# The start of a fused convolution and MLP kernel: absolute values, softmax steps and weight loads issued in another order

## The chip, the cores and the metric

One core of one Trainium2 chip runs the whole kernel. The metric is the device time of one execution in microseconds (us), the median of several runs; lower is better.

The engines that matter: TensorE (PE, its weight loads are PEld) multiplies matrices into PSUM; VectorE (DVE) and ScalarE (ACT) do elementwise work; SyncE (SP) issues most DMAs and GpSimd (POOL) a few. Each engine works through its own instructions strictly in the order in which they were issued, and waits where one of them needs a result of another engine.

## The reference

```python
w = softmax(weight_gen, axis=-1)                 # (4, 4096, 8, 7)
x_unf = causal windows of 7 rows of x            # x: (4, 4096, 192)
out = einsum('bshk,bskhg->bshg', w, x_unf)       # a convolution with weights per position and head
h = out.reshape(16384, 192) @ w_in               # (192, 2048)
g = s * relu(h)**2 + b
result = g @ w_out                               # (2048, 192)
```

Weights arrive as doubles (pairs of 32-bit words); the rest is float32.

## The kernel before

The 16384 tokens are cut into 32 groups of 512. For each group the convolution is worked out in "pieces" (softmax, products with the seven taps, sums, a transposition, a split of the result in a high and a low part), and then the MLP runs over the 2048 hidden columns. Precision comes from splitting: weights and activations are held as a high and a low part in the fp32r format, and the products high x high, low x high and high x low are added up in PSUM.

The hidden columns are cut into eight chunks of 256 (`wc[0]` to `wc[7]`). In the first group each chunk's weights have to be converted from doubles before they can be used. `convert(i)` is a generator of four steps, and `ahead(i, n)` runs the next n steps of chunk i:

1. ScalarE takes the absolute value (L228) into the tile `t`, once all of the chunk's weights have landed.
2. VectorE clamps and shifts it (L231, L235) and puts the float together in `r` (L239); ScalarE casts the high part (L243).
3. VectorE takes the exponent (L246) and scales the low word into `v` (L250). `t` is free after that.
4. TensorE forms the low part in PSUM (L260 to L262), ScalarE casts it (L263).

The first group runs as eight turns of a loop, i = 0 to 7 (L681 on). Turn i is: first product of chunk i on TensorE (`mm1_pair`, L527); ScalarE takes relu (L556), square (L558) and, after the low part of chunk i+1 (L263), the cast `gh` (L562); step 2 and 3 of chunk i+2 and step 1 of chunk i+3; second product of chunk i-1 (`mm2_pair`, L596), which alternates `gh` and `gl` as operands; pieces of the second group's convolution as the table `beside` says; then VectorE's `gl` (L568) for chunk i. So on TensorE the order is: first product of i, conversion of i+1 (L260), second product of i-1.

The order in the program is the order on each engine (`manual_schedule`). The pieces of a group are numbered 0 softmax_a (L382, L384), 1 exp (ACT, L390), 2 softmax_b (L395 to L399), 3 to 6 products (L413), 7 to 10 sums (L424), 11 last sum (L432), 12 transposes (L443, L448), 13 split_hi (two ACT casts, L455), 14 split_lo (two DVE subtractions, L461, and DMAs). After turn 7 the column sums of the second weights go to PSUM (L296, in the tile tagged h1), VectorE makes `bias` from them (L304, L305), and the steady loop starts with `mm1_quad` (L545), whose second output again needs the buffer h1.

In the steady loop each step n does the first product of a pair of chunks (`mm1_quad`, L545), relu and square, the second product of the pair before (`mm2_quad`, L614, which works on output tiles 0 and 2 first and then on 1 and 3), and pieces of the next group. At the start of a group, `scale` (L626, L632) brings the outputs of the group before from PSUM to SBUF, which also frees the four PSUM banks for the new group.

Weights come in pairs of chunks, `load_weights(k)`, into two buffers `r`: four transfers of first weights (L189), eight small ones (L198, on the queue named `side`), and one or two of second weights (L206).

Pair 1 is loaded right after pair 0 and the second group's `weight_gen`; pair 2 overwrites the buffer of pair 0 and so is issued when chunk 1 has been read.

Of the kernel before, what the change touches and what calls it, by code (L numbers as in the profile page):

```python
# [20 lines left out]
def dynamic_conv_then_relu2_mlp(  # L21
# [28 lines left out]
    P = 128  # L50
# [24 lines left out]
    rows = ctx.enter_context(tc.tile_pool(name="rows", bufs=1))  # L75
# [5 lines left out]
    yp = ctx.enter_context(tc.tile_pool(name="yp", bufs=2))  # L81
    ps_h = ctx.enter_context(tc.tile_pool(name="ps_h", bufs=1, space=bass.MemoryType.PSUM))
# [136 lines left out]
    def convert(i):  # L219
# [6 lines left out]
        t = raw.tile([P, CW], U32, tag="t", name="t", bufs=1)  # L226
# [38 lines left out]

    spare = const.tile([P, 16], F32, name="spare")
# [220 lines left out]
    def run_pieces(g, a, b):  # L487

        if g < NG:
            if g not in pieces_t:  # L490
                pieces_t[g] = conv_pieces(g)
            for f in pieces_t[g][a:b]:
                f()
# [159 lines left out]
    with tc.manual_schedule():  # L653
        constants()
        nc.scalar.activation(out=spare[:, 0:1], in_=ones_f[:, 0:1], func=AF.Exp)
        load_rows(0)
        load_weights(0, (0,), nc.gpsimd)
        load_weights(0, (1,), nc.gpsimd)
        load_gen(1)
        load_weights(1)  # L660
# [6 lines left out]
        def ahead(i, n):  # L667
            for _ in range(n if i < NC else 0):
                next(parts[i])
# [10 lines left out]
        beside = ((2, 4), (4, 5), (5, 7), (7, 8), (8, 10), (10, 12), (12, 14), (14, 15))  # L680
        for i in range(NC):  # L681
            n, p = divmod(i, 2)
            mm1_pair(n, p, (0, 2, 1) if i == 0 else (0, 1, 2))
            if i == 0:
                ahead(1, 2)
            relu2(n, [p], lambda: ahead(i + 1, 1))
            if i == 0:
                ahead(2, 1)
                run_pieces(1, 0, 2)
            ahead(i + 2, 2)  # L690
            ahead(i + 3, 1)
            if i == NC - 1:
                sums = column_sums()
            if i > 0:
                mm2_pair((i - 1) // 2, (i - 1) % 2)
            run_pieces(1, *beside[i])
            low_g(n, p)
            if i == 0:
                load_weights(2)
            if i == NC - 1:  # L700
                set_bias(sums)
            if i == 1:
                load_weights(3)
            if i == 4:
                load(2)
        run_pieces(2, 0, 3)
        last = NG * NQ - 1
        for n in range(NQ, last + 1):
# [14 lines left out]
            if k == 0:  # L723
                scale(g - 1, (0, 2, 1, 3))
                store(g - 1, 0, NT)
            low_g(n, 1)
# [38 lines left out]
```

## Time and profile before

| | |
|---|---|
| median of 3 runs | 1182.03 us (1180.51 to 1182.61) |
| the profiled execution's own time | 1182.32 us |
| its span in the trace | 1180.6 us |
| TensorE matmul busy | 99% of the span |
| VectorE, ScalarE busy | 79%, 70% |
| DMA, mean over the span | 43 GB/s |

The span is the time from the first instruction to the last; the execution's own time lies 1.7 us above it. TensorE is busy nearly all the time, so what it still waits for is looked up in the view of waits, and where that happens in the timeline.

### The profile page before, as it was taken

To read this page: it belongs to the slowest core of one execution; us is meant where nothing else is said; L and a number is where in the kernel's file an instruction comes from. 1 tells how busy PE (TensorE), PEld (TensorE's weight loads), DVE (VectorE), ACT (ScalarE), POOL (GpSimd) and SP (SyncE) were. 2 spreads that over 40 slices of the span, in tenths; PEclk is the share of its full clock that TensorE was granted. 3 is DMA by queue.
4 is the path that set the end of the run, shared out by engine and by line. 5 is a ranking of instruction groups with operands and counts; after the bars stand their busy time and mean duration, and the time that the engine had idled before them with its cause. 6 is when DMAs were issued, how large, how long until landed. Compare 5 with 4: busy or idle time off the path is not lost.

```text
span 1180.6 us, 30020 instructions
## 1 busy us (share of the span) xinstructions
PE 1163.3 (99%) x12736; PEld 1047.2 (89%) x12736; DVE 931.9 (79%) x1356; ACT 828.1 (70%) x894; POOL 13.9 (1%) x38
## 2 busy tenths in 40 slices
PE   7999999999999999999999999999999999999997
PEld 5688998998999999989989999999899899999996
DVE  7978887777888777798777788777788877788843
ACT  5767776776776767767767767677677677677674
POOL 2000000000000000000000000000000000000000
PEclk9999999999999999999999999999999999999999
DMA  7411122222112222112222112222212222211110
GB/s 191 106 32 37 32 38 47 46 33 46 25 36 46 46 33 46 27 34 46 46 36 42 31 34 42 46 46 33 41 28 38 46 46 33 46 25 36 24 24 15
DMA packets 171290, 50.36 MB, mean 43 GB/s; under 512 B 160212, under 2 KB 163924, under 8 KB 171156
## 3 DMA queue, kind: packets, MB, share of 16 engines
q1 hardware_dynamic: 170644, 48.18, 21.9%
q8 instruction: 100, 1.64, 0.6%
q0 software_dynamic: 512, 0.26, 0.1%
q14 instruction: 34, 0.28, 0.1%
HBM read 27.70 MB, written 12.58 MB: 34 GB/s over the span
## 4 chain that ended last, share of the span: by engine, by line
PE 95%; DVE 1%; ACT 1%; DMA 1%; SPq 1%; issue 0%; DVEq 0%
PE po L614 47%; PE ph L545 44%; PE po L596 2%; PE ph L527 1%; DMA r<-in_moe_w_in_dram 1%; PE ph L260 1%; DVE gl L568 0%; ACT r L558 0%; SPq L198 0%; SPq L189 0%; ACT gh L562 0%; ACT r L556 0%; PE ph L296 0%; DMA r<-in_moe_w_out_dram 0%; SPq L122 0%
## 5 line engine op out<-in xcount | busy, mean ns | idle before, releaser
L614 PE MATMUL po<-wc,gh 64*128 64x384 f32 x3936 | 571.7, 356 | 0.0
L614 PE MATMUL po<-wc,gl 64*128 64x192 f32 x3936 | 495.2, 248 | 0.8 <-DVE gl L568 0.8
L568 DVE TENSOR_TENSOR gl<-r,gh 128x1024 fp32r<-128x1024 f32 x256 | 313.0, 1223 | 222.4 <-ACT gh L562 214.3
L556 ACT ACTIVATE r<-ph 128x1024 f32<-128x1024 f32 x256 | 249.1, 1024 | 311.9 <-PE ph L545 302.7
L614 PEld LDWEIGHTS po<-wc,gl 64*128 64x128 f32 x3936 | 375.5, 187 | 6.4 <-DVE gl L568 1.0
L614 PEld LDWEIGHTS po<-wc,gh 64*128 64x128 f32 x3936 | 369.7, 184 | 5.4
L545 PE MATMUL ph<-xa,wc 64*128 64x512 f32 x2976 | 369.8, 394 | 0.0
L545 PEld LDWEIGHTS ph<-xa,wc 64*128 64x128 f32 x2976 | 270.6, 185 | 55.0 <-issue 0.2
L562 ACT CAST gh<-r 128x1024 fp32r<-128x1024 f32 x256 | 268.8, 1050 | 7.9
L558 ACT ACTIVATE r<-r 128x1024 f32<-128x1024 f32 x256 | 270.8, 1058 | 0.3
L545 PE MATMUL ph<-xb,wc 64*128 64x512 f32 x1488 | 192.2, 390 | 0.0
L413 DVE TENSOR_TENSOR pr<-xt,w 128x1536 f32<-128x1536 f32 (+1 forms) x124 | 187.6, 1553 | 1.3
L545 PEld LDWEIGHTS ph<-xb,wc 64*128 64x128 f32 x1488 | 139.7, 184 | 32.8
L424 DVE TENSOR_TENSOR pr<-pr 128x1536 f32<-128x1536 f32 (+1 forms) x124 | 140.7, 1155 | 2.1
L626 DVE SCALAR_TENSOR_TENSOR u<-po,s_sb,bias 128x192 f32<-128x192 f32 x128 | 49.8, 409 | 1.6 <-PE po L596 1.6
L632 DVE SCALAR_TENSOR_TENSOR y<-po,s_sb,u 128x192 f32<-128x192 f32 x128 | 49.7, 408 | 0.1
L432 DVE TENSOR_TENSOR acc<-pr 128x768 f32<-128x768 f32 x31 | 29.7, 958 | 1.1
L443 DVE STREAM_TRANSPOSE xT<-acc 128x128 f32<-128x128 f32 x124 | 27.6, 280 | 1.0
L448 DVE STREAM_TRANSPOSE xT<-acc 128x128 f32<-128x128 f32 x124 | 26.3, 269 | 0.0
L596 PE MATMUL po<-wc,gh 128*128 128x384 f32 x80 | 25.5, 379 | 0.1
L596 PE MATMUL po<-wc,gl 128*128 128x192 f32 x80 | 21.1, 264 | 3.4 <-DVE gl L568 3.4
L461 DVE TENSOR_TENSOR xa<-xT,xa 128x512 fp32r<-128x512 f32 x31 | 21.2, 685 | 0.0
(60 smaller groups left out, 351.7 us busy)
## 6 DMA issues: line engine op xcount, KB each, us to landing
xt<-in_x_dram SPq DMA_DIRECT2D x120, 132.0 KB, 3.3
out_dram<-y SPq DMA_DIRECT2D x124, 96.0 KB, 1.9
xb<-xb SPq DMA_DIRECT2D x124, 64.0 KB, 2.3
wg<-in_weight_gen_dram SPq DMA_DIRECT2D x124, 28.0 KB, 2.6
r<-in_moe_w_out_dram SPq DMA_DIRECT2D x8, 384.0 KB, 3.6
r<-in_moe_w_in_dram SPq DMA_DIRECT2D x12, 128.0 KB, 3.1
r<-in_moe_w_in_dram SPq DMA_DIRECT2D x24, 32.0 KB, 1.9
xr<-in_x_dram SPq DMA_DIRECT2D x1, 672.0 KB
```

The source lines that it names most:

```text
L413: nc.vector.tensor_tensor(out=pr[:, k0:k1, :, h * G:(h + 1) * G], in0=bass.AP(xs.tensor, xs.offset, [xs.ap[0], [FQ, n], [FQ, J], [1, G]]), ...
L424: nc.vector.tensor_tensor(out=pr[:, o:o + n], in0=pr[:, o:o + n], in1=pr[:, a:a + n], op=ALU.add)
L432: nc.vector.tensor_tensor(out=acc, in0=pr[:, 0], in1=pr[:, 2], op=ALU.add)
L545: nc.tensor.matmul(out=h_t[n, p][:, j], lhsT=w1(2 * k + p, part, block, j, rows), rhs=v[rows], start=(at < 2 and c == 0), stop=(at >= 4 an ...
L556: nc.scalar.activation(out=r[p], in_=h_t.pop((n, p)), func=AF.Relu)
L558: nc.scalar.activation(out=r[p], in_=r[p], func=AF.Square)
L562: nc.scalar.copy(out=gh, in_=r[p])
L568: nc.vector.tensor_tensor(out=gl, in0=sq, in1=gh.bitcast(F32), op=ALU.subtract)
L596: nc.tensor.matmul(**m)
L614: nc.tensor.matmul(**m)
L626: nc.vector.scalar_tensor_tensor(out=u[i], in0=o_t[g][tiles[i]][:, 1, :], scalar=s_sb, in1=bias, op0=ALU.mult, op1=ALU.add,)
L632: nc.vector.scalar_tensor_tensor(out=y[:, t], in0=o_t[g][t][:, 0, :], scalar=s_sb, in1=u[i - 1], op0=ALU.mult, op1=ALU.add,)
```

## The change

- Odd chunks take their tile `t` (step 1 of a conversion) from the pool `rows`; so even and odd chunks have a buffer each, where there was one. The pool `rows` is made after the others.
- Step 1 of chunk 2 is issued ahead of relu of turn 0, and ahead of the cast of chunk 1's high part.
- In turn 1 the first product takes its operands in the order high x high, high x low, low x high, as turn 0 already did; the low part of the weights is needed last.
- The second group's pieces are spread anew over the eight turns: turn 0 does only softmax_a; exp and softmax_b are in turn 1, and turn 6 does the last three sums, the transposes and split_hi.
- The weights of pair 1 are issued on SP ahead of the second group's `weight_gen`; the eight small transfers of pair 2 are issued by POOL.
- The scaling of the first group's output is split in two halves, tiles 0 and 2, then 1 and 3; the second `gl` stands between them.
- The dummy exp that loads ScalarE's table writes to `bias` in place of a tile of its own.

```diff
-    rows = ctx.enter_context(tc.tile_pool(name="rows", bufs=1))
...
     yp = ctx.enter_context(tc.tile_pool(name="yp", bufs=2))
+    rows = ctx.enter_context(tc.tile_pool(name="rows", bufs=1))
...
-        t = raw.tile([P, CW], U32, tag="t", name="t", bufs=1)
+        t = (rows if i % 2 else raw).tile([P, CW], U32, tag="t", name="t", bufs=1)
...
+        load_weights(1)
         load_gen(1)
-        load_weights(1)
...
-        beside = ((2, 4), (4, 5), (5, 7), (7, 8), (8, 10), (10, 12), (12, 14), (14, 15))
+        beside = ((0, 1), (1, 3), (3, 4), (4, 5), (5, 7), (7, 8), (8, 14), (14, 15))
         for i in range(NC):
             n, p = divmod(i, 2)
-            mm1_pair(n, p, (0, 2, 1) if i == 0 else (0, 1, 2))
+            mm1_pair(n, p, (0, 2, 1) if i < 2 else (0, 1, 2))
             if i == 0:
+                ahead(2, 1)
                 ahead(1, 2)
             relu2(n, [p], lambda: ahead(i + 1, 1))
-            if i == 0:
-                ahead(2, 1)
-                run_pieces(1, 0, 2)
...
-                load_weights(2)
+                load_weights(2, side=nc.gpsimd)
...
-            if k == 0:
+            if n == NQ:
+                scale(0, (0, 2))
+                low_g(n, 1)
+                scale(0, (1, 3))
+                store(0, 0, NT)
+            elif k == 0:
                 scale(g - 1, (0, 2, 1, 3))
                 store(g - 1, 0, NT)
-            low_g(n, 1)
+            if n > NQ:
+                low_g(n, 1)
```

ScalarE at the start of the loop, before. `wc_0` to `wc_3` are the chunks' converted weights, `r_121` holds chunks 0 and 1, `r_153` chunks 2 and 3; L228 is step 1, L243 the high part, L263 the low part, L556 to L562 are relu, square and `gh`, L390 is exp.

```order
L243 CAST wc_0_91<-r_121 128x768
L228 ACTIVATE t_289<-r_121 128x768
L263 CAST wc_0_91<-ph_291 128x768
L243 CAST wc_1_92<-r_121 128x768
L556 ACTIVATE r_319<-ph_299 128x1024
L558 ACTIVATE r_319<-r_319 128x1024
L263 CAST wc_1_92<-ph_322 128x768
L562 CAST gh_330<-r_319 128x1024
L228 ACTIVATE t_332<-r_153 128x768
L390 ACTIVATE e_336<-e_336 128x224
L243 CAST wc_2_93<-r_153 128x768
L228 ACTIVATE t_346<-r_153 128x768
```

The same stretch of ScalarE in the changed kernel, where `r_120` holds chunks 0 and 1 and `r_147` chunks 2 and 3 (lines are two lower from here on).

```order
L243 CAST wc_0_91<-r_120 128x768
L228 ACTIVATE t_288<-r_120 128x768
L263 CAST wc_0_91<-ph_290 128x768
L228 ACTIVATE t_311<-r_147 128x768
L243 CAST wc_1_92<-r_120 128x768
L554 ACTIVATE r_320<-ph_298 128x1024
L556 ACTIVATE r_320<-r_320 128x1024
L263 CAST wc_1_92<-ph_323 128x768
L560 CAST gh_331<-r_320 128x1024
L243 CAST wc_2_93<-r_147 128x768
L228 ACTIVATE t_340<-r_147 128x768
L554 ACTIVATE r_376<-ph_363 128x1024
```

Chunk 2's absolute value has moved up past five instructions, to ahead of chunk 1's high part; exp has left this stretch and now comes after chunk 4's absolute value, ahead of the relu of turn 2. On VectorE, chunk 2's five conversion steps now follow chunk 1's directly, then softmax_a, `gl` of turn 0, chunk 3's conversion, softmax_b, `gl` of turn 1.

VectorE from the conversion of chunk 7 on, before. L424 and L432 are sums of the second group's convolution, L443 and L448 its transposes, L568 is `gl`, L461 split_lo, L304 and L305 make the bias.

```order
L250 SCALAR_TENSOR_TENSOR v_652<-r_432,t_589 128x768
L424 TENSOR_TENSOR pr_354<-pr_354 128x768
L432 TENSOR_TENSOR acc_671<-pr_354 128x768
L568 TENSOR_TENSOR gl_673<-r_634,gh_645 128x1024
L443 STREAM_TRANSPOSE xT_717<-acc_671 128x128 x4
L448 STREAM_TRANSPOSE xT_717<-acc_671 128x128 x4
L568 TENSOR_TENSOR gl_730<-r_688,gh_699 128x1024
L461 TENSOR_TENSOR xb_727<-xT_717,xb_727 128x512
L461 TENSOR_TENSOR xa_726<-xT_717,xa_726 128x512
L568 TENSOR_TENSOR gl_789<-r_745,gh_748 128x1024
L304 TENSOR_SCALAR cs_791<-ph_750,b_sb_100 128x192
L305 SCALAR_TENSOR_TENSOR bias_106<-ph_750,b_sb_100,cs_791 128x192
```

The same stretch of VectorE in the changed kernel; the first row is again the end of chunk 7's conversion.

```order
L250 SCALAR_TENSOR_TENSOR v_648<-r_428,t_585 128x768
L422 TENSOR_TENSOR pr_494<-pr_494 128x1536
L566 TENSOR_TENSOR gl_667<-r_630,gh_641 128x1024
L422 TENSOR_TENSOR pr_494<-pr_494 128x768 x3
L430 TENSOR_TENSOR acc_714<-pr_494 128x768
L441 STREAM_TRANSPOSE xT_716<-acc_714 128x128 x4
L446 STREAM_TRANSPOSE xT_716<-acc_714 128x128 x4
L566 TENSOR_TENSOR gl_729<-r_682,gh_693 128x1024
L459 TENSOR_TENSOR xb_726<-xT_716,xb_726 128x512
L459 TENSOR_TENSOR xa_725<-xT_716,xa_725 128x512
L566 TENSOR_TENSOR gl_788<-r_744,gh_747 128x1024
L302 TENSOR_SCALAR cs_790<-ph_749,b_sb_100 128x192
```

Three sums and the last one now stand behind the `gl` of turn 5 and ahead of the transposes, with no conversion left in between; before, they were done in turns 4 and 5.

VectorE at the first step of the steady loop, before: `gl`, the eight scaling steps of the first group's output (u and y for four tiles), the second `gl`.

```order
L568 TENSOR_TENSOR gl_884<-r_855,gh_860 128x1024
L626 SCALAR_TENSOR_TENSOR u_886<-po_408,s_sb_99,bias_106 128x192
L626 SCALAR_TENSOR_TENSOR u_887<-po_410,s_sb_99,bias_106 128x192
L632 SCALAR_TENSOR_TENSOR y_412<-po_408,s_sb_99,u_886 128x192
L626 SCALAR_TENSOR_TENSOR u_888<-po_409,s_sb_99,bias_106 128x192
L632 SCALAR_TENSOR_TENSOR y_412<-po_410,s_sb_99,u_887 128x192
L626 SCALAR_TENSOR_TENSOR u_889<-po_411,s_sb_99,bias_106 128x192
L632 SCALAR_TENSOR_TENSOR y_412<-po_409,s_sb_99,u_888 128x192
L632 SCALAR_TENSOR_TENSOR y_412<-po_411,s_sb_99,u_889 128x192
L568 TENSOR_TENSOR gl_899<-r_857,gh_863 128x1024
```

The same in the changed kernel, where `po_398` to `po_401` are the output tiles 0 to 3.

```order
L566 TENSOR_TENSOR gl_883<-r_854,gh_859 128x1024
L624 SCALAR_TENSOR_TENSOR u_885<-po_398,s_sb_99,bias_106 128x192
L624 SCALAR_TENSOR_TENSOR u_886<-po_400,s_sb_99,bias_106 128x192
L630 SCALAR_TENSOR_TENSOR y_402<-po_398,s_sb_99,u_885 128x192
L630 SCALAR_TENSOR_TENSOR y_402<-po_400,s_sb_99,u_886 128x192
L566 TENSOR_TENSOR gl_891<-r_856,gh_862 128x1024
L624 SCALAR_TENSOR_TENSOR u_893<-po_399,s_sb_99,bias_106 128x192
L624 SCALAR_TENSOR_TENSOR u_894<-po_401,s_sb_99,bias_106 128x192
L630 SCALAR_TENSOR_TENSOR y_402<-po_399,s_sb_99,u_893 128x192
L630 SCALAR_TENSOR_TENSOR y_402<-po_401,s_sb_99,u_894 128x192
```

The second `gl` has moved ahead of four of the eight scaling steps, those of tiles 1 and 3. TensorE's instructions stand in the same order in both kernels, but for the operands of turn 1.

## Rows read from the trace of the kernel before

**Rows 1.** The page: busy time, share of the span, instructions of each engine.

```profile
PE 1163.3 (99%) x12736; PEld 1047.2 (89%) x12736; DVE 931.9 (79%) x1356; ACT 828.1 (70%) x894; POOL 13.9 (1%) x38
```

**Rows 2.** Waits of PE: who waited for whom, total us, times, longest us.

```profile
PE po L596 <- DVE gl L568: 3.4, 2, 2.6
...
PE ph L527 <- ACT wc L263: 0.4, 1, 0.4
```

**Rows 3.** One stretch: PE, PEld, DVE, ACT, POOL busy, granted clock, DMA, GB/s.

```profile
36.00:39.00 3.00, 3.00 (x13) 3.00 (x13) 2.83 (x5) 1.15 (x2) 0.00 (x0) 0.54 0.00 0
```

**Rows 4.** Timeline, 21 to 42 us: start, busy, engine, line, [idle before <- releaser].

```profile
21.09 0.91 ACT L243 CAST wc<-r 128x768 fp32r<-128x768 f32 x1 [0.99 <-DVE r L239]
...
22.55 0.38 DVE L382 TENSOR_REDUCE mx<-wg 128x32 f32<-128x224 f32 x1
...
25.84 0.89 ACT L228 ACTIVATE t<-r 128x768 f32<-128x768 f32 x1
...
26.75 0.56 DVE L231 TENSOR_SCALAR t<-t 128x768 f32<-128x768 f32 x1 [3.40 <-ACT t L228]
...
29.23 0.92 PE L260 MATMUL ph<-r,eye_f 128*128 128x384 f32 x2 [2.09 <-issue]
...
29.82 0.96 DVE L250 SCALAR_TENSOR_TENSOR v<-r,t 128x768 fp32r<-128x768 uint32 x1
...
41.27 0.94 PE L260 MATMUL ph<-r,eye_f 128*128 128x384 f32 x2
```

**Rows 5.** Timeline of undisturbed turns, 40 to 55 us.

```profile
40.34 1.22 DVE L568 TENSOR_TENSOR gl<-r,gh 128x1024 fp32r<-128x1024 f32 x1
...
47.73 1.22 DVE L568 TENSOR_TENSOR gl<-r,gh 128x1024 fp32r<-128x1024 f32 x1
...
48.12 0.94 PE L260 MATMUL ph<-r,eye_f 128*128 128x384 f32 x2
48.23 1.02 ACT L556 ACTIVATE r<-ph 128x1024 f32<-128x1024 f32 x1 [1.23 <-PE ph L527]
...
50.28 0.34 PE L596 MATMUL po<-wc,gh 128*128 128x384 f32 x1
...
52.93 0.92 ACT L228 ACTIVATE t<-r 128x768 f32<-128x768 f32 x1
...
54.26 1.22 DVE L568 TENSOR_TENSOR gl<-r,gh 128x1024 fp32r<-128x1024 f32 x1
...
54.96 0.94 PE L260 MATMUL ph<-r,eye_f 128*128 128x384 f32 x2
```

**Rows 6.** Timeline: exp of the third group and what follows softmax_b.

```profile
81.61 0.39 ACT L390 ACTIVATE e<-e 128x224 f32<-128x224 f32 x1 [2.79 <-DVE e L384]
...
83.48 1.76 DVE L413 TENSOR_TENSOR pr<-xt,w 128x1536 f32<-128x1536 f32 x1
```

**Rows 7.** Timeline of SP's queue: first issue of weight pair 2.

```profile
23.89 1.74 SPq L189 DMA_DIRECT2D r<-in_moe_w_in_dram  x4
```

**Rows 8.** Line L198 on POOL: ns min/median/max of an issue; us to landing.

```profile
L198 POOL DMA_DIRECT2D r<-in_moe_w_in_dram x16: 484/484/642, 1.5 to 10.5; - x16
...
DMA to landing us min/median/max: 2.8/4.3/5.2
```

**Rows 9.** Timeline: split_hi's second cast, bias, first `mm1_quad`; sums to `gl`.

```profile
73.19 0.62 ACT L455 CAST xa<-xT 128x512 fp32r<-128x512 f32 x1
...
80.44 0.42 DVE L305 SCALAR_TENSOR_TENSOR bias<-ph,b_sb,cs 128x192 f32<-128x192 f32 x1
...
80.75 3.05 PE L545 MATMUL ph<-xa,wc 64*128 64x512 f32 x24
...
100.02 2.81 DVE L424 TENSOR_TENSOR pr<-pr 128x768 f32<-128x768 f32 x3
...
105.45 1.18 DVE L568 TENSOR_TENSOR gl<-r,gh 128x1024 fp32r<-128x1024 f32 x1
```

**Rows 10.** Timeline: TensorE in the first second product of the steady loop.

```profile
93.56 0.36 PE L614 MATMUL po<-wc,gl 64*128 64x192 f32 x2 [0.77 <-DVE gl L568]
```

More of the change, by code (lines that the diff above doesn't have):

```diff
@@ L264, in convert @@
         yield
-    spare = const.tile([P, 16], F32, name="spare")
     def awake():
@@ L654, in dynamic_conv_then_relu2_mlp @@
         constants()
-        nc.scalar.activation(out=spare[:, 0:1], in_=ones_f[:, 0:1], func=AF.Exp)
+        nc.scalar.activation(out=bias[:, 0:1], in_=ones_f[:, 0:1], func=AF.Exp)
         load_rows(0)
```

## The prediction

> **What bounds the kernel now.** I read the busy shares first: TensorE is busy for 99% of the span [rows 1], so time can be won only where it still waits or runs slowly, and a change elsewhere matters only if it makes TensorE wait. The view of waits names the places: TensorE's second product waits for VectorE's `gl` twice, 3.4 us in all, 2.6 the longest, and the first product once for the low part of the weights, 0.4 us [rows 2]. The timeline shows where: between the conversion of chunk 2 (L260 at 29.23, after 2.09 us of idleness) and that of chunk 3 (41.27), which is one turn of the first group's loop [rows 4]. An undisturbed turn takes 48.12 to 54.96, 6.84 us [rows 5]; this one took 12.04. The windows view adds that behind its waits the granted clock was 0.54 from 36 to 39 us, so nearly the lower of the two levels, 1.2 GHz, while TensorE was busy all the time [rows 3]. After 41 us the view of waits has only one more for TensorE, 0.77 us at 93.56 [rows 10]. So a turn brought forward there brings the end forward by as much, if nothing new is late.
>
> **The change part by part.**
>
> *Chunk 2's absolute value earlier (gain).* VectorE stood idle for 3.40 us before chunk 2's conversion, waiting for step 1 on ScalarE, which came only at 25.84 [rows 4]. ScalarE was idle for 0.99 us ahead of the cast at 21.09, and the absolute value takes 0.89 [rows 4]: it fits into that hole, so it costs the instructions queued behind it (the high part of chunk 1, relu) nothing, if the weights have landed by about 20.1. VectorE then starts chunk 2 where softmax_a stood, at 22.55, and reaches `v` 3.07 us later (26.75 to 29.82 in rows 4), at 25.62, done at 26.58. The high part can take ScalarE's place at 25.84. The separate `t` for odd chunks removes the wait of one chunk's absolute value for the `v` of the chunk before; here VectorE's own order hides it, so I count it at nothing.
>
> So L260 of chunk 2 no longer waits: 2.09 us [rows 4]. The new order of operands in turn 1 removes the wait for the low part, 0.4 us [rows 2]; it leaves two matmuls in place of four behind it. L260 of chunk 2 thus stands at 29.23 - 2.5 = 26.7.
>
> *softmax_b and products out of turn 0 (gain).* `gl` of turn 0 stood behind them. Now VectorE does `v` to 26.58, two softmax_a steps of some 0.4 us (0.38 for the first, rows 4), and `gl` 1.22: ready at 28.6. TensorE wants it one matmul (0.2) into the second product, which starts 2.16 us after L260 (48.12 to 50.28 in rows 5): at 29.0. No wait, with 0.4 us to spare; what is late next is `gl` of turn 1, below. Without waits the turn takes 6.84 in place of 12.04, so 5.2 us are won. That includes the slow clock: no idleness above 0.5 us is left in front of it, so I take the upper level, 2.4 GHz, throughout.
> Gains to here: 2.1 + 0.4 + 5.2 = 7.7 us.
>
> *exp behind chunk 4's absolute value (cost).* `gl` of turn 1 now waits for softmax_b, that for exp, and exp stands in ScalarE's queue behind chunk 4's absolute value. ScalarE: high part of chunk 2 at 25.84, 0.91; absolute value of chunk 3, 0.9; relu of turn 1 at 27.7; from a relu to the absolute value behind it 4.70 (48.23 to 52.93, rows 5): 32.4; 0.92 for it; exp at 33.3; from exp to the instruction behind softmax_b 1.87 [rows 6]: `gl` starts at 35.2, ready at 36.4. TensorE wants it at 26.7 + 6.84 + 2.16 + 0.2 = 35.9. Wait: 0.5 us; bounds 0, if handovers overlap, and 1.4, if chunk 4's loads are 0.9 late. Behind it on VectorE stands chunk 4's conversion; the turns that follow move with it.
>
> *Pieces spread anew (turns 2 to 5: nothing).* VectorE's turn from `gl` to `gl` is 6.53 with a sum or one product (47.73 to 54.26), and 7.39 with two products (40.34 to 47.73) [rows 5], where TensorE's is 6.84. After two turns of the first kind and one of the second VectorE has used 20.45 of TensorE's 20.52 us: the cover holds, by 0.07. If it fails, each turn costs what VectorE is over; I bound this by 0 and 0.5.
>
> *Sums and transposes in turn 6 (cost).* Count from TensorE's first use of `gl` in turn 1. VectorE began that `gl` at -1.22, begins the `gl` of turn 5 at 3 x 6.53 + 7.39 - 1.22 = 25.8, is done at 27.0, does sums and transposes for 5.43 (100.02 to 105.45, rows 9), to 32.4. Then ScalarE does split_hi, two casts of 0.62 [rows 9], to 33.7, and only behind them relu of turn 7. TensorE has ended the first product of turn 7 at 4 x 6.84 + 4.6 = 32.0, the 4.6 being from the `gl` matmul to the next relu (6.84 - 2.16 - 0.2 + 0.1, rows 5). So relu of turn 7, and with it `gl` and the bias, are 1.7 us later against TensorE. The bias was ready at 80.86; `mm1_quad` wants the buffer h1 after a quarter of its 24 matmuls, 80.75 + 0.76 = 81.51 [rows 9]. Of the 1.7 us 0.65 are covered: a new wait of 1.0 us. Bounds: 0, if handovers are tighter than busy times added up, and 1.7.
>
> *Scaling in two halves (gain).* The 0.77 us of rows 10 go, since `gl` no longer stands behind the scaling of tiles 1 and 3. These tiles' banks are wanted a quarter into the same product, and their scaling now ends later; between 0 and 0.77 I take 0.5.
>
> *Loads.* On SP pair 1's fourteen transfers move ahead of four of `weight_gen`, which softmax_a wants only at 26.6. POOL takes over eight small transfers of pair 2. SP began this pair at 23.89 [rows 7]; POOL takes 0.484 us for each issue [rows 8], so the last goes out at 27.3 and lands 2.8 to 5.2 later [rows 8]: 30.1 to 32.5, wanted by the absolute value at 32.4. No cost taken; the bound is 0.1 by these rows. One POOL issue of sixteen took 642 ns in place of 484 [rows 8].
> On this the Trainium skill speaks against the change: "SBUF — State Buffer", section "SBUF: two separate sides", says that while VectorE runs an operation in a mode that takes both ports, GpSimd can't write descriptors, so a DMA from its queue waits. The one long issue, 158 ns over, may be such a case; fifteen of sixteen show none. By the rule the result would be that of the first rival.
>
> *The rest.* The dummy exp, the pool's place: no instruction more or less, nothing.
>
> Sum: 7.7 - 0.5 - 1.0 + 0.5 = 6.7 us. The profiled execution took 1182.32 in all, with a span of 1180.6; so 1175.6, and as this execution lies 0.3 above the median, 1175.3.
>
> **The rivals.**
>
> *POOL's transfers are late.* Conversions use L231, L235 and L246, each taken at the 0.56 us of the first [rows 4]. If each of the three holds POOL once, the last transfer lands 1.7 later, at up to 34.2, 1.8 us after the absolute value of chunk 4 wants it; exp, softmax_b, `gl` and TensorE follow: 1177.1. For it: ScalarE works in order, nothing gets past the absolute value. Against it: 484 ns as median with VectorE at work.
>
> *Chunk 2's weights aren't there at 20.1, so the change doesn't do what it says.* The trace of before shows only that they were there at 25.84. If they come 3 us late, ScalarE holds the high part of chunk 1 for 3 us, and 3 of the 7.7 are gone: 1178.3. Against it: they are issued earlier than before.
>
> *VectorE gives all of it back.* If VectorE were the true bound of the whole first group, TensorE's gain would return as waits, 1182. Against it: VectorE was idle 3.40 us in this stretch alone [rows 4] and its turns are shorter than TensorE's but for one.
>
> *Slower.* The one mechanism with a price: ScalarE stuck at chunk 4's absolute value behind POOL's loads, while relu of turn 2 and all later work queue behind it. Every us past 32.4 costs one; from 39.1 on (32.4 + 6.7) the kernel is slower, and with loads landed at 42 it takes 1182.0 - 6.7 + 9.6 = 1184.9. For it: POOL's first issue must wait for the buffer's readers. Against it: landing took 5.2 at most.
>
> **How the numbers follow.** Forecast 0.72, POOL late 0.10, chunk 2 late 0.08, no change 0.06, slower 0.04. The forecast's own range: none of the new waits and all of the 0.77 give 8.5 us, 1173.5; waits of 1.4, 1.7, 0.5 and no gain in scaling give 7.7 - 3.6 = 4.1, 1177.9. The range of 8 in 10 goes a little beyond both, 1173.0 to 1178.8, and takes in the first two rivals. About 0.2% (2.4 us, so 1179.7) can be told from no change. Faster: 0.72 + 0.10 + 0.08 = 0.90, less 0.01 for later weights; same 0.07; slower 0.04.
>
> **What would show it.** In the changed profile: chunk 2's absolute value at about 20.1 and L260 of chunk 2 near 26.7 without idleness (first gain); no wait above 0.5 us before the second product of turn 0 and a granted clock of 1.0 up to 40 us (second); L260 of chunk 3 at about 33.5; a wait of about 0.5 for `gl` in turn 1; a wait of about 1 us in the first `mm1_quad` for the bias; 0.77 at the start of the steady loop shrunk to about 0.3. I am wrong if VectorE waits for ScalarE before chunk 4's conversion by more than 2 us, or if TensorE's turns 2 to 5 are longer than 6.84.

## The result, and the profile after

The changed kernel takes 1169.44 us (median of 4 runs, 1168.69 to 1170.88) against 1182.32 for the kernel before; the ratio is 0.9895, with a 95% interval of 0.9878 to 0.9913. The forecast was 1175.3, with a range of 1173.0 to 1178.8. So the kernel gained 12.9 us, where 6.7 were worked out. The profiled execution took 1168.69 us, its span 1167.0. Lines of the changed file stand two lower from the convolution's tiles on: L525 and L543 are the first products, L594 and L612 the second ones, L566 is `gl`.

The page's busy times, answering [rows 1]: TensorE's share is still 99%, but PE is busy 9.1 us less for the same 12736 instructions. A kernel that only waits less, at the same clock, keeps its busy time.

```profile
PE 1154.2 (99%) x12736; PEld 1136.0 (97%) x12736; DVE 931.9 (80%) x1356; ACT 828.0 (71%) x894; POOL 18.0 (2%) x46
```

TensorE's waits in the changed kernel, answering [rows 2]: `gl` 2.2 instead of 3.4 us, the 0.4 for the weights' low part gone, 0.2 for the bias new. One of the two waits for `gl` in each sum, 0.82 us, stands at the kernel's end (1170.89 before, 1157.41 now) and is not touched by the change.

```profile
PE po L594 <- DVE gl L566: 2.2, 2, 1.4
...
PE ph L543 <- DVE bias L303: 0.2, 1, 0.2
```

The windows view of 36 to 39 us, answering [rows 3], with the granted clock third from the right: 1.00 now, 0.54 before.

```profile
36.00:39.00 3.00, 1.71 (x12) 1.71 (x13) 2.86 (x5) 2.29 (x3) 0.00 (x0) 1.00 0.70 193
```

The changed kernel's timeline of the first group, answering [rows 4, 5, 7, 8]:

```profile
19.91 0.91 ACT L228 ACTIVATE t<-r 128x768 f32<-128x768 f32 x1
...
24.35 4.01 POOL L198 DMA_DIRECT2D r<-in_moe_w_in_dram  x8 [12.83 <-PE ph L262]
...
26.55 0.94 PE L260 MATMUL ph<-r,eye_f 128*128 128x384 f32 x2
...
27.36 1.22 DVE L566 TENSOR_TENSOR gl<-r,gh 128x1024 fp32r<-128x1024 f32 x1
...
33.37 0.94 PE L260 MATMUL ph<-r,eye_f 128*128 128x384 f32 x2
33.48 0.89 ACT L228 ACTIVATE t<-r 128x768 f32<-128x768 f32 x1 [1.55 <-DMA r<-in_moe_w_in_dram]
34.27 0.38 ACT L388 ACTIVATE e<-e 128x224 f32<-128x224 f32 x1
...
34.68 0.39 DVE L393 TENSOR_REDUCE sm<-e 128x32 f32<-128x224 f32 x1 [2.38 <-ACT e L388]
...
36.02 1.22 DVE L566 TENSOR_TENSOR gl<-r,gh 128x1024 fp32r<-128x1024 f32 x1
...
37.29 0.36 PE L594 MATMUL po<-wc,gl 128*128 128x192 f32 x1 [1.43 <-DVE gl L566]
...
41.89 0.94 PE L260 MATMUL ph<-r,eye_f 128*128 128x384 f32 x2
...
48.72 0.94 PE L260 MATMUL ph<-r,eye_f 128*128 128x384 f32 x2
```

Chunk 2's absolute value starts at 19.91 without a wait, its conversion (L260) at 26.55, chunk 3's at 33.37, chunk 4's at 41.89, where it was 48.12 [rows 5]: 6.2 us won. New is ScalarE's wait of 1.55 us for chunk 4's weights, behind it VectorE's of 2.38 for exp, and behind that TensorE's 1.43 for `gl`. From there a turn takes 6.83.

The steady loop's start in the changed kernel, TensorE's rows, answering [rows 9, 10]; each group of xa rows begins one `mm1_quad`:

```profile
74.51 0.97 PE L543 MATMUL ph<-xa,wc 64*128 64x512 f32 x6
75.63 2.35 PE L543 MATMUL ph<-xa,wc 64*128 64x512 f32 x18 [0.15 <-DVE bias L303]
...
81.75 3.07 PE L543 MATMUL ph<-xa,wc 64*128 64x512 f32 x24
...
91.16 0.41 PE L543 MATMUL ph<-xa,wc 64*128 64x512 f32 x1
...
99.88 0.41 PE L543 MATMUL ph<-xa,wc 64*128 64x512 f32 x1
...
108.60 0.41 PE L543 MATMUL ph<-xa,wc 64*128 64x512 f32 x1
```

And the same stretch of the kernel before:

```profile
87.60 3.05 PE L545 MATMUL ph<-xa,wc 64*128 64x512 f32 x24
...
97.48 2.98 PE L545 MATMUL ph<-xa,wc 64*128 64x512 f32 x24
...
101.69 0.34 PE L614 MATMUL po<-wc,gh 64*128 64x384 f32 x2
...
106.27 2.98 PE L545 MATMUL ph<-xa,wc 64*128 64x512 f32 x24
...
115.05 2.27 PE L545 MATMUL ph<-xa,wc 64*128 64x512 f32 x18
```

The third `mm1_quad` begins at 91.16 instead of 97.48: 6.3 us won, close to the 6.7 of the forecast. But then a step takes 8.72 (91.16 to 99.88) where it took 8.78 (97.48 to 106.27), with no wait in either. Some 122 steps follow: 122 x 0.06 = 7.3 us, more than half of the gain, and none of it worked out in the forecast. Grouped by line from 400 to 1000 us, the last number but one being the mean ns of one matmul, the kernel before:

```profile
L545 PE MATMUL ph<-xa,wc 64*128 64x512 f32 x1632 | 202.7, 394 | 0.0
L545 PE MATMUL ph<-xb,wc 64*128 64x512 f32 x820 | 106.0, 390 | 0.0
```

and the changed kernel:

```profile
L543 PE MATMUL ph<-xa,wc 64*128 64x512 f32 x1649 | 212.2, 391 | 0.0
L543 PE MATMUL ph<-xb,wc 64*128 64x512 f32 x823 | 115.0, 388 | 0.0
```

The same matmul of the same shape, at the same granted clock of 1.00, is 2 to 3 ns shorter. The experiments ask why.

### The profile page after: what moved, and what is told of

Its sections match the earlier page's. It is cut to its first block, busy times and chain, and to the rows that moved or that the text cites. A ratio compares the mean times of both kernels' runs of the same rounds, so it can differ in the third digit from the quotient of the medians.

```text
span 1167.0 us, 30031 instructions
## 1 busy us (share of the span) xinstructions
PE 1154.2 (99%) x12736; PEld 1136.0 (97%) x12736; DVE 931.9 (80%) x1356; ACT 828.0 (71%) x894; POOL 18.0 (2%) x46
## 4 chain that ended last, share of the span: by engine, by line
PE 92%; DVE 4%; DMA 1%; ACT 1%; POOL 1%; issue 0%; DVEq 0%; ACTq 0%; POOLq 0%
PE po L612 46%; PE ph L543 45%; DMA r<-in_moe_w_in_dram 1%; DVE gl L566 1%; POOL r L198 1%; DVE pr L411 1%; DVE r L239 0%; DVE v L250 0%; DVE pr L422 0%; ACT gh L560 0%; PE po L594 0%; ACT r L556 0%; ACT r L554 0%; DVE t L246 0%; PE ph L525 0%
## 5 line engine op out<-in xcount | busy, mean ns | idle before, releaser
L612 PE MATMUL po<-wc,gh 64*128 64x384 f32 x3936 | 588.1, 356 | 0.1
L612 PE MATMUL po<-wc,gl 64*128 64x192 f32 x3936 | 577.0, 247 | 0.0
L612 PEld LDWEIGHTS po<-wc,gh 64*128 64x128 f32 x3936 | 574.0, 184 | 0.5 <-DVE y L630 0.3
L612 PEld LDWEIGHTS po<-wc,gl 64*128 64x128 f32 x3936 | 569.1, 188 | 0.0
L566 DVE TENSOR_TENSOR gl<-r,gh 128x1024 fp32r<-128x1024 f32 x256 | 313.0, 1223 | 209.7 <-ACT gh L560 203.4
L543 PE MATMUL ph<-xa,wc 64*128 64x512 f32 x2976 | 383.0, 391 | 0.2 <-DVE bias L303 0.2
L543 PEld LDWEIGHTS ph<-xa,wc 64*128 64x128 f32 x2976 | 338.9, 185 | 1.3 <-PE ph L543 0.6
L556 ACT ACTIVATE r<-r 128x1024 f32<-128x1024 f32 x256 | 270.8, 1058 | 0.3
L543 PE MATMUL ph<-xb,wc 64*128 64x512 f32 x1488 | 207.6, 388 | 0.0
L543 PEld LDWEIGHTS ph<-xb,wc 64*128 64x128 f32 x1488 | 182.3, 185 | 0.0
L594 PE MATMUL po<-wc,gh 128*128 128x384 f32 x80 | 23.9, 362 | 0.1
L594 PE MATMUL po<-wc,gl 128*128 128x192 f32 x80 | 20.2, 253 | 2.2 <-DVE gl L566 2.2
L159 POOL MEMSET xt<- 1x288 f32 x16 | 5.3, 333 | 1042.7 <-DVE xT L441 1042.1
```

The source lines that it names most:

```text
L543: nc.tensor.matmul(out=h_t[n, p][:, j], lhsT=w1(2 * k + p, part, block, j, rows), rhs=v[rows], start=(at < 2 and c == 0), stop=(at >= 4 an ...
L556: nc.scalar.activation(out=r[p], in_=r[p], func=AF.Square)
L566: nc.vector.tensor_tensor(out=gl, in0=sq, in1=gh.bitcast(F32), op=ALU.subtract)
L594: nc.tensor.matmul(**m)
L612: nc.tensor.matmul(**m)
```

## The experiments

**First theory: how the two halves of the array stand to each other.** In the changed kernel the matmuls of the array's rows 0 to 63 and 64 to 127 start half a matmul's time apart (the single xa row at 91.16), and weight loads (PEld) are busy 97% of the span; in the kernel before both halves start together, 89% [rows 1]. The split scaling seemed to set them apart. Its rival: the halves don't matter. Four runs put it to the test.

*e1_scale_old*: the changed kernel with the old order.

```diff
-            if n == NQ:
-                scale(0, (0, 2))
-                low_g(n, 1)
-                scale(0, (1, 3))
-                store(0, 0, NT)
-            elif k == 0:
+            if k == 0:
                 scale(g - 1, (0, 2, 1, 3))
                 store(g - 1, 0, NT)
-            if n > NQ:
-                low_g(n, 1)
+            low_g(n, 1)
```

> The changed kernel with the scaling of the first group's output in its old place, all eight steps ahead of the second gl; everything else stays changed. Theory (row halves): the changed kernel's steady loop is faster because TensorE's two halves of 64 rows run half a period apart, and this was set off by the two banks that came free 0.4 us apart in the first mm2_quad. Here both halves wait for the same gl, so they start together: weight loads busy 91% as before, a step of 8.78 us in place of 8.72, about 1176 us (1169.4 + 7, and up to 0.5 for the wait that is back). Rival 1 (addresses: the pool moved and the dummy tile gone): 1169.5 to 1170. Rival 2 (what is left of the start decides): also about 1170.

1170.98 us, ratio 0.9898 (0.9883 to 0.9912). The page's busy times show the halves together again, PEld at 89%:

```profile
PE 1153.7 (99%) x12736; PEld 1043.4 (89%) x12736; DVE 931.7 (80%) x1356; ACT 827.8 (71%) x894; POOL 18.0 (2%) x46
```

Yet TensorE's rows show the step at 8.72 (92.28 to 101.00). Of the scaling itself, the wait of [rows 10] is back (0.76 us).

```profile
92.28 2.95 PE L543 MATMUL ph<-xa,wc 64*128 64x512 f32 x24
...
101.00 1.34 PE L543 MATMUL ph<-xa,wc 64*128 64x512 f32 x10
```

*e2_scale_only*: the opposite edit, the split scaling alone in the kernel before.

```diff
-            if k == 0:
+            if n == NQ:
+                scale(0, (0, 2))
+                low_g(n, 1)
+                scale(0, (1, 3))
+                store(0, 0, NT)
+            elif k == 0:
                 scale(g - 1, (0, 2, 1, 3))
                 store(g - 1, 0, NT)
-            low_g(n, 1)
+            if n > NQ:
+                low_g(n, 1)
```

> The kernel before with only the scaling split in two halves and the second gl between them. Theory (row halves): the halves come apart, steps of 8.72 us, so 7 us and 0.5 for the wait that goes: about 1175 us, weight loads 97% busy. Rival 1 (addresses) and rival 2 (the start): at most 0.5 us less than before, about 1182.

1182.82 us, 0.9996 (0.9985 to 1.0007). The halves are apart, PEld 97%, and the step is 8.78 (98.07 to 106.85):

```profile
98.07 2.98 PE L545 MATMUL ph<-xa,wc 64*128 64x512 f32 x23
...
106.85 2.98 PE L545 MATMUL ph<-xa,wc 64*128 64x512 f32 x23
```

*e3_scale_reversed*: the changed kernel, the second half of the scaling in reverse.

```diff
-                scale(0, (1, 3))
+                scale(0, (3, 1))
```

> The changed kernel with tiles 3 and 1 scaled in this order in place of 1 and 3: the same instructions, two of them swapped. Theory (row halves): TensorE's first matmul of this stretch, that of the first half on tile 1, now waits for the bank that comes free last, so the second half's can start with it; no offset, steps of 8.78 us, about 1176 us. Rival 1 and rival 2: 1169.4, no difference.

1171.85 us, 0.9899 (0.9883 to 0.9916): together (PEld 89%), and the step 8.72. In its profiled execution the turn from chunk 3's conversion to chunk 4's took 10.7 us at a lower clock, of which more in the last section.

*e4_lag_once*: the kernel before, one half's sixteen matmuls one place later in a quarter of one `mm2_quad`.

```diff
-            for c in range(8):
...
+            steps = [(c, i) for c in range(8) for i in range(2)]
+            if n == NQ + 1 and at == 0:
+                steps.sort(key=lambda s: (s[0] + s[1], s[1]))
+            for c, i in steps:
```

> The kernel before with one thing changed: in one quarter of one mm2_quad, the one after the first, the second half's sixteen matmuls are issued one place later against the first half's. No wait, address or other engine is touched. Theory (row halves), if any offset once made is kept: steps of 8.72 us from there on, about 1175.5 us. If an offset fades or only one of half a period counts: 1182.3 and steps of 8.78 us. Rivals 1 and 2: 1182.3.

1184.21 us, 1.0005 (0.9996 to 1.0015). The lag did not persist (PEld 89%, step 8.78), so this run alone says little. With e1 to e3 the theory falls: with the halves together or apart, variants of the changed kernel take 8.72 and variants of the kernel before 8.78.

**Second theory: where the tiles lie.** What still sets the two apart in the steady loop is the layout of SBUF, the on-chip memory that holds the tiles. The change dropped the tile `spare` (64 bytes a partition) and moved the pool `rows` (7680 bytes) behind the others, so all tiles from the convolution's on lie 7744 bytes lower, and the converted weights stay. A cross of four runs separates layout and order.

*e5_before_moved*: the old order at the new addresses.

```diff
-    rows = ctx.enter_context(tc.tile_pool(name="rows", bufs=1))
...
     yp = ctx.enter_context(tc.tile_pool(name="yp", bufs=2))
+    rows = ctx.enter_context(tc.tile_pool(name="rows", bufs=1))
...
-    spare = const.tile([P, 16], F32, name="spare")
+    spare = rows.tile([P, 16], F32, name="spare")
```

> The kernel before, word for word in its order; only the pool of the first group's rows is made behind all others and the 64-byte tile of the dummy exp stands in it, so that every tile from the raw weights to the outputs lies at the address that it has in the changed kernel (xa 149696 instead of 157440; from the convolution's tiles on all lie 7744 bytes lower). Theory: the steady loop's pace goes by the addresses of its tiles: a step takes 8.72 us instead of 8.78, some 120 steps give 7 us, and the time is 1175 to 1177 with the old start (second quad at 97.4). Rival: something that the changed start leaves behind sets the pace: nothing changes, 1182 to 1184, step 8.78.

1175.64 us, 0.9935 (0.9920 to 0.9950). TensorE's rows: 97.72 to 106.44 is 8.72, of which the first products (to the first L614 row) take 4.16 instead of 4.21.

```profile
97.72 2.95 PE L545 MATMUL ph<-xa,wc 64*128 64x512 f32 x24
...
101.88 0.34 PE L614 MATMUL po<-wc,gh 64*128 64x384 f32 x2
...
106.44 0.88 PE L545 MATMUL ph<-xa,wc 64*128 64x512 f32 x6
```

*e6_after_unmoved*: the new order at the old addresses.

```diff
     xin = ctx.enter_context(tc.tile_pool(name="xin", bufs=2))
+    rows = ctx.enter_context(tc.tile_pool(name="rows", bufs=1))
...
-    rows = ctx.enter_context(tc.tile_pool(name="rows", bufs=1))
+    odd = ctx.enter_context(tc.tile_pool(name="odd", bufs=1))
...
     bias = const.tile([P, D], F32, name="bias")
+    spare = const.tile([P, 16], F32, name="spare")
...
-        t = (rows if i % 2 else raw).tile([P, CW], U32, tag="t", name="t", bufs=1)
+        t = (odd if i % 2 else raw).tile([P, CW], U32, tag="t", name="t", bufs=1)
```

> The changed kernel, its order kept; the 64 bytes and the rows' pool are put back where they were, so that the tiles from the raw weights to the outputs lie at the addresses of the kernel before (only the odd chunks' t is in a pool behind). Theory of the addresses: step 8.78, time 1176 to 1177.5, which is what the changed start alone gives (6.3 us). Rival: 1169 to 1171, step 8.72.

1177.01 us, 0.9948 (0.9934 to 0.9963), step 8.78. The two halves of the cross add up: against 1183.20, the median of before beside them, the addresses alone give 7.6 us and the order alone 6.2, together 13.8 (both changes: 12.9 by the medians, 13.6 by the two profiled executions, 1182.32 and 1168.69).

*e7_rows_last* (only the pool moved, by the first edit of e5) and *e8_no_spare* (only the 64 bytes dropped) split the layout. The edit of e8:

```diff
-    spare = const.tile([P, 16], F32, name="spare")
...
-        nc.scalar.activation(out=spare[:, 0:1], in_=ones_f[:, 0:1], func=AF.Exp)
+        nc.scalar.activation(out=bias[:, 0:1], in_=ones_f[:, 0:1], func=AF.Exp)
```

> The kernel before with the pool of the rows made last and the 64-byte tile left in its place: tiles from the convolution's on lie 7680 bytes lower, the weights where they were. By the theory of the addresses the large move alone makes the step 8.72 and the time 1175 to 1177 if the 64 bytes play no part, and 1182 to 1184 if it is they that matter. Rival: 1182 to 1184.

1183.04 us, 0.9994 (0.9984 to 1.0003), step 8.78.

> The kernel before without the 64-byte tile (the dummy exp writes to the bias): everything behind it lies 64 bytes lower. By the theory of the addresses 1175 to 1177 if the 64 bytes matter, and 1182 to 1184 if the 7680 bytes of the rows' pool do. Rival: 1182 to 1184.

1175.53 us, 0.9938 (0.9922 to 0.9955), step 8.72. So the 64 bytes do it, and the pool's move does nothing.

**Which tile.** An unused tile in the changed kernel, put ahead of the tiles of one pool or another, shifts all behind it by 64 bytes. *e9_pad_xtp* has it ahead of xa and xb; *e10_pad_act* and *e11_pad_gp* have the same line for `act` and `gp`, *e12_pad_all* for `const`, ahead of the weights.

```diff
     xtp = ctx.enter_context(tc.tile_pool(name="xtp", bufs=2))
+    xtp.tile([P, 16], F32, tag="pad", name="pad", bufs=1)
```

> The changed kernel with an unused tile of 64 bytes ahead of xa and xb: xa, xb, the relu's r, gh, gl and y lie at a multiple of 128 bytes again, as in the kernel before; the weights' raw tiles and the convolution's stay 64 bytes off it. If it is what TensorE reads and writes in the steady loop that counts, all 7.3 us come back: 1176 to 1177.5, step 8.78. If it is the tiles ahead of these (raw weights, inputs, products of the convolution), 1169 to 1171.

1178.73 us, 0.9962 (0.9949 to 0.9975), step 8.78: the faster pace is lost.

> The same with the unused tile behind xa and xb: these stay 64 bytes off, and only r, gh, gl and y lie at a multiple of 128. If the place of mm1_quad's moving operand counts (its 24 products with xa 2.79 us instead of 2.82, its 12 with xb 1.37 instead of 1.39, some 0.05 us of the step's 0.06), the time stays within 2 us of the changed kernel: 1169 to 1173. If it is r, gh or gl, 1175 to 1177.5.

1170.67 us, 0.9903 (0.9889 to 0.9918), step 8.72. Between these two only xa and xb move: here they decide.

> The same with the unused tile behind r: only gh, gl and y lie at a multiple of 128. If gh and gl count by themselves, as mm2_quad's stationary operand (4.58 instead of 4.56 us a step), the time is about 2 us above the changed kernel, 1171 to 1173; if they don't, 1169 to 1171; if all of it hangs on them, 1175 to 1177.5. Against the run before it, it tells r apart.

1170.11 us, 0.9898 (0.9883 to 0.9912), step 8.72.

> The changed kernel with the unused tile of 64 bytes ahead of the converted weights: these and all behind them lie 64 bytes higher, so that the weights are 64 bytes off a multiple of 128 and all else is on it. If only the distance of the weights from the other operands counts (two reads of one parity that collide), the pace stays: 1169 to 1171. If each tile's own place counts, 1176 to 1177.5, or another pace again where the weights' place counts too.

1169.83 us, 0.9897 (0.9882 to 0.9913), step 8.72. xa and xb lie where they lay in e9, but the weights have moved with them: it is the distance that counts. (The tiles between the weights and xa moved in e12 as well; that the other end of the distance is the weights is argued, not shown: `mm1_quad` reads nothing else.)

**Which distance.** *e16_pad_32* and *e17_pad_192* are e9 with `[P, 8]` and `[P, 48]` in the tile. *e18_x_alone* is the kernel before with 64 bytes ahead of xa and xb and 64 behind them:

```diff
     xtp = ctx.enter_context(tc.tile_pool(name="xtp", bufs=2))
+    xtp.tile([P, 16], F32, tag="pad", name="pad", bufs=1)
     act = ctx.enter_context(tc.tile_pool(name="act", bufs=3))
+    act.tile([P, 16], F32, tag="pad", name="pad", bufs=1)
```

> The changed kernel with an unused tile of 32 bytes ahead of xa and xb, which then lie 96 bytes off a multiple of 128 (the weights lie on one, xa and xb were 64 off it). If the two reads collide where their 64-byte blocks have the same parity, a row that begins in the middle of a block meets the weights' parity in half of its length: step between 8.72 and 8.78, 1169 to 1173. If only an equal remainder of 128 counts: step 8.72, 1169 to 1171. If any place but 64 off is slow: step 8.78, 1176 to 1178.

1179.24 us, 0.9959 (0.9946 to 0.9971), step 8.79.

> The changed kernel with an unused tile of 192 bytes ahead of xa and xb: they lie at a multiple of 128 bytes, as the weights do, and at the weights' own remainder of 256 (in the kernel before the two were 128 apart by that measure). If the remainder of 128 decides, this is as slow as the kernel before: step 8.78, 1176 to 1179. If it is the remainder of 256 and only half a period apart collides, step 8.72, 1169 to 1171.

1165.35 us (1163.29 to 1167.29), 0.9851 (0.9833 to 0.9870): neither expectation, and the lowest median of all, though its interval overlaps that of e13 below.

> The kernel before, its order kept, with one unused tile of 64 bytes ahead of xa and xb and one behind them: xa and xb alone lie 64 bytes off a multiple of 128, the weights, the relu's r, gh, gl and y on one as before. If these two tiles' place is the whole cause of the steady loop's gain: step 8.72, 1175 to 1177. If it takes another tile's move besides (the raw weights, r, gh or gl): step 8.78, 1182 to 1184.

1176.51 us, 0.9956 (0.9941 to 0.9972). The time is the one expected of xa and xb as the whole cause, and the trace says otherwise. TensorE's rows of e18:

```profile
98.07 3.06 PE L547 MATMUL ph<-xa,wc 64*128 64x512 f32 x24
...
102.28 0.41 PE L616 MATMUL po<-wc,gh 64*128 64x384 f32 x2
...
106.81 0.49 PE L547 MATMUL ph<-xa,wc 64*128 64x512 f32 x2
```

The first products take 4.21, as slow as before; the second ones 4.53 instead of 4.58. So xa and xb, 64 off a multiple of 128, bring nothing here, and what moved by 128 (r, gh, gl, y) brings 0.05 in `mm2_quad`. Of the 6.6 us below the kernel before beside it this pace gives some 4 (122 steps at 8.747 instead of 8.780); the trace does not settle the rest. TensorE's rows of e17 show both products short, 4.17 and 4.52:

```profile
95.41 3.00 PE L544 MATMUL ph<-xa,wc 64*128 64x512 f32 x24
...
99.58 0.37 PE L613 MATMUL po<-wc,gh 64*128 64x384 f32 x2
...
104.10 1.15 PE L544 MATMUL ph<-xa,wc 64*128 64x512 f32 x8
```

The table sets the places against the two products; the places are the tiles' addresses in the built programs less the weights', as a remainder of 256 bytes; the times are means of 24 to 54 steps between 300 and 1000 us, read as above.

| kernels | xa, xb | `mm1_quad`, us | r, gh, gl, y | `mm2_quad`, us |
|---|---|---|---|---|
| before, e6, e7, e9 | 128 | 4.20 to 4.21 | 128 | 4.57 to 4.58 |
| after, e5, e8, e12 | 64 | 4.15 to 4.16 | 64 | 4.56 to 4.57 |
| e10 (e11: r at 64) | 64 | 4.14 to 4.15 | 128 | 4.57 |
| e16 | 96 | 4.22 | 96 | 4.56 |
| e17 | 0 | 4.15 | 0 | 4.53 |
| e18 | 192 | 4.22 | 0 | 4.53 |

The expectations spoke of the remainder of 128; by that e17 had to be slow and e18's first products short, and both were not. So that account falls. By 256, `mm1_quad` is short at 0 and 64 and long at 96, 128 and 192; `mm2_quad` is shortest at 0. This was read off these runs after the fact: none was made to test it, and a longer period than 256 would fit them as well.

**The start, one term each.**

*e13_exp_first*: exp ahead of chunk 4's absolute value.

```diff
-        beside = ((0, 1), (1, 3), (3, 4), (4, 5), (5, 7), (7, 8), (8, 14), (14, 15))
+        beside = ((0, 1), (2, 3), (3, 4), (4, 5), (5, 7), (7, 8), (8, 14), (14, 15))
...
+            if i == 1:
+                run_pieces(1, 1, 2)
             ahead(i + 3, 1)
```

> The changed kernel; in turn 1 the next group's exp stands ahead of chunk 4's absolute value (before that chunk's small blocks, which GpSimd sends for and whose landing held ScalarE for 1.55 us at 33.48, have to be there). Expected: the exp starts near 32 instead of 34.27, its sums and gl(1) follow earlier, and TensorE's wait of 1.43 us for gl before the products at 37.29 goes; the time is 0.8 to 1.5 us below the changed kernel, 1168 to 1168.7. Rival: chunk 4's own steps are late in its place and a later turn waits as long: 1169 to 1170.5.

1167.09 us (1166.84 to 1168.06), 0.9860 (0.9845 to 0.9875): below the expected 1168 to 1168.7, and 2.2 below e14 on the same chip. In the profiled executions of these two the third `mm1_quad` begins at 90.30 and 91.76. ScalarE's rows: it still waits for chunk 4's weights, but exp is done before.

```profile
33.11 0.40 ACT L388 ACTIVATE e<-e 128x224 f32<-128x224 f32 x1
35.29 0.91 ACT L228 ACTIVATE t<-r 128x768 f32<-128x768 f32 x1 [1.79 <-DMA r<-in_moe_w_in_dram]
```

TensorE's rows: chunk 3's conversion to chunk 4's is an undisturbed turn, 6.82, where the changed kernel has 8.52 (33.37 to 41.89).

```profile
34.67 0.94 PE L260 MATMUL ph<-r,eye_f 128*128 128x384 f32 x2
...
41.49 0.94 PE L260 MATMUL ph<-r,eye_f 128*128 128x384 f32 x2
```

*e14_loads_on_sp*: pair 2's small blocks on SP's queue.

```diff
-                load_weights(2, side=nc.gpsimd)
+                load_weights(2)
```

> The changed kernel with the small blocks of pair 2 on SP's queue as before. If GpSimd's issue (eight from 24.35 on, 4.01 us) is what made chunk 4's absolute value wait 1.55 us for its data, the wait is gone and the time 0.5 to 1.5 us lower. Rival: on SP they stand behind the others as in the kernel before and land later: chunk 4's absolute value waits longer and the time is up to 2 us higher.

1169.31 us, 0.9877 (0.9863 to 0.9892): no difference from the changed kernel that the intervals can tell. ScalarE's wait is as long; what lands last is now the second weights:

```profile
34.16 0.90 ACT L228 ACTIVATE t<-r 128x768 f32<-128x768 f32 x1 [1.55 <-DMA r<-in_moe_w_out_dram]
```

In the changed kernel's trace the last second weights landed at 32.31 and GpSimd's last block at 32.99. With all of pair 2 on one queue the second weights are issued later and land last, as late. So this move gains nothing; what GpSimd's queue costs by itself e14 does not tell.

*e15_abs_back*: chunk 2's absolute value behind the first relu again.

```diff
             if i == 0:
-                ahead(2, 1)
                 ahead(1, 2)
             relu2(n, [p], lambda: ahead(i + 1, 1))
+            if i == 0:
+                ahead(2, 1)
```

> The changed kernel with chunk 2's absolute value behind the first relu's three operations again, where the kernel before has it; the order of the next group's pieces stays changed. By the prediction's working the conversion of chunk 2 starts 2 to 2.5 us later and the time is 1171.5 to 1172. Rival: only the moved pieces counted and this one move counts nothing: 1169 to 1170.5.

1172.01 us, 0.9901 (0.9886 to 0.9916): 2.7 above e14, which ran on the same chip. In the timeline the absolute value stands at 26.51, and TensorE's idleness is back:

```profile
26.51 0.89 ACT L228 ACTIVATE t<-r 128x768 f32<-128x768 f32 x1
...
29.68 1.38 PE L260 MATMUL ph<-r,eye_f 128*128 128x384 f32 x2 [2.33 <-issue]
```

The 2.7 is a balance of three terms beside e14's trace: chunk 2's conversion starts 2.44 later (27.24 to 29.68); the turn behind it takes 8.75 instead of 6.83, with a granted clock of 0.50 from 30 to 33 us; and the next takes 6.83 instead of 8.51, since `gl` is now in time.

e13 and e17 both beat the two kernels; their edits are in different places, and both at once was not run.

## Why the prediction was wrong

**The step that failed is "The rest": "The dummy exp, the pool's place: no instruction more or less, nothing."** It priced a layout by its instructions. e5, e7 and e8 show that dropping the 64 bytes of the dummy exp's tile is worth 7.6 to 7.7 us by itself, more than all the reordering, and the pool's place indeed nothing. No part of the range was kept for it: every rival and bound stood in the first 100 us, and a change of 0.7% in the pace of the remaining 1070 us weighs as much as all of them.

The rest held nearly: the reordering was forecast at 6.7 us, and e6, which has it at the old addresses, lies 6.2 below the kernel before. That it came so near is in part luck, as the terms show. One reading was wrong without harm: behind 41 us TensorE waits not once more but twice, the second time at the kernel's end (0.82 at 1170.89).

- *Chunk 2's absolute value earlier (gain)*: right. It stood at 19.91 (20.1 forecast), the conversion at 26.55 (26.7). e15 puts the price of taking it back at 2.7 (2.5 forecast), but as a balance that also holds the slow clock and the wait for `gl`.
- *softmax_b and products out of turn 0 (gain)*: right. No wait, clock 1.00, chunk 3's conversion at 33.37 (33.5 forecast).
- *exp behind chunk 4's absolute value (cost)*: the mechanism right, the size not: TensorE waited 1.43 instead of 0.5, by the upper bound of 1.4, and the turn took 8.52 instead of 6.83. The late data of that bound came true. So did a sign by which the prediction called itself wrong, VectorE waiting more than 2 us for ScalarE ahead of chunk 4's conversion: it was 2.38, ahead of softmax_b and with it of `gl` and that conversion. e13 takes exp out of that place, and TensorE's wait goes.
- *Loads*: wrong by about 1 us. The chain put the last landing at 30.1 to 32.5; in the trace it is at 32.99, 5.13 behind its issue, and ScalarE went on at 33.48. GpSimd began at 24.35, not 23.9. By the Trainium skill ("SBUF — State Buffer", section "SBUF: two separate sides") GpSimd can't write descriptors while VectorE runs an operation that takes both ports. The issues show little of it: eight took 4.01 us, 0.50 each beside the 0.484 of [rows 8], so 0.14 in all, and only one operation of the kind that the first rival prices (L246 at 24.67) ran beside them. So data came late, as in the first rival, but by these issues hardly for its reason.
- *Pieces spread anew*: right, 6.83 a turn (41.89 to 48.72).
- *Sums and transposes in turn 6 (cost)*: right in kind, too large. The first `mm1_quad` takes 7.24 (74.51 to 81.75), 0.4 over the 6.85 of before (80.75 to 87.60), 0.15 of it a wait for the bias; 1.0 was forecast.
- *Scaling in two halves (gain)*: right. From the second to the third `mm1_quad` it is 9.41 instead of 9.88: 0.47 (0.5 forecast).

The sum of the measured terms: 48.12 to 41.89 gives 6.23, less 0.39, plus 0.47: 6.3, which is what the third `mm1_quad` shows (these are stretches of one timeline, so they must add up). Behind it stand two misses of opposite sign: about 1.2 too little for exp behind the loads (1.69 instead of 0.5) and 0.6 too much for the sums and transposes.

## What to carry to other kernels

A tile that is added, dropped or resized moves every tile behind it, and with TensorE busy 99% of the time the place of its operands is a term of the sum: after any change of layout compare the mean ns of a steady matmul before and after, ahead of every wait. To find out whether order or layout made a gain, build the cross: the old order at the new addresses and the new order at the old ones. And put work that needs no new data ahead of work that waits for a load, on an engine that runs in order (e13).

## What the runs showed of the hardware

*The pace of a matmul goes by where its operands lie.* A 64-row first product with xa, 512 columns of four bytes, took 394 ns or 391 by its operands' place; an `mm1_quad` of 36 such matmuls 4.21 or 4.15 us. Over both products the table spans 1.3% of a step, from 8.67 in e17 to 8.79 in e16. The Trainium skill ("TensorE: Matmul & The Clock Gate", section "Step-by-step: what each phase is for") says that TensorE has two independent read ports, so that loading the next weights takes no read bandwidth from the running matmul. The weight loads beside these matmuls do read a tile whose distance from xa sets the pace, so here either the two reads are not wholly independent, or another access is in the way; no run tells these apart. The traces narrow it down: where VectorE stands idle, from one xa matmul to the sixth behind it takes 703 ns before and 695 after (means of 80 and 40 places from 300 to 1000 us), so VectorE's accesses are not needed for the difference; and e10 and e11 moved the tiles that ScalarE writes (r, gh) and left `mm1_quad` as short. Whether r, gh, gl or y makes `mm2_quad` short at 0 stays open as well.

*Halves of the array together or apart cost the same*: 8.72 both in e1 (together) and after (apart), 8.78 both before and in e2.

*A slightly longer wait can cost much more.* In the profiled execution of e17 chunk 4's data came later and TensorE waited for `gl` as the row below shows, 2.73 us:

```profile
39.08 0.53 PE L595 MATMUL po<-wc,gl 128*128 128x192 f32 x1 [2.73 <-DVE gl L567]
```

In the window behind it the granted clock was 0.50, the lower of the two levels (1.2 GHz), while TensorE was busy:

```profile
39.00:45.00 6.00, 5.92 (x20) 5.53 (x21) 5.72 (x8) 2.83 (x4) 0.00 (x0) 0.50 0.55 176
```

Behind the changed kernel's 1.43 us the clock stayed at 1.00 (above). Nor is e17 alone. Eleven profiled executions have this wait with exp behind chunk 4's absolute value. In the four with 1.42 to 1.49 us (after, e1, e6, e14) the clock from 39 to 42 us was 1.00, and chunk 3's conversion to chunk 4's took 8.5 to 8.6 us. Of the seven with 1.79 to 2.73 us, six had a clock of 0.50 to 0.70 there and 10.5 to 12.8 us (e3, e9, e10, e12, e16, e17); e11, with 2.12, kept 1.00 and took 9.2. So this wait's price hangs on when chunk 4's weights land, and these executions hold up to 4.3 us of it; the step, read far from the start, does not. With exp first (e13) the wait was not there.
